# Splitting float32 weights into two float16 halves: GpSimd's subtraction replaced by two TensorE products, and the planner's table drawn anew

## The chip, the cores and the metric

One core of a Trainium2 chip runs the kernel. The metric is device microseconds of one execution, as the median of three runs. Engine names are those of the profile: PE is TensorE (matmuls), PEld its weight loads, DVE is VectorE, ACT is ScalarE, POOL is GpSimd, SP is SyncE, which here issues all DMAs.

## The reference

The inputs are float64. Attention with 8 batches, 8 heads, 576 tokens and a head width of 64 keeps for each query only the 32 largest scores; its output x (4608 tokens by 512) goes through a layer that takes the largest of three products and multiplies it by a fourth matrix.

```
scores = matmul(q, k.T) / sqrt(D)
kth    = partition(scores, -32)[..., -32:-31]
scores = where(scores >= kth, scores, -1e9)
attn   = exp(scores - max) / (sum + 1e-9)
x      = (attn @ v) reshaped to [4608, 512]
h      = max(max(x @ w1, x @ w2), x @ w3)      # w: [512, 768]
out    = h @ w_out                             # [768, 512]
```

## The kernel before

**Units of attention.** The work is cut into units of 128 queries of two heads; 144 units make the 8 batches. A unit goes through all engines: PE makes the scores in PSUM (L518), ACT copies them to SBUF as `ssb` (L526), DVE takes the 8 largest of each of 7 stretches (L535) and a pivot from them (L549 to L567), ACT takes signs against the pivot (L574), POOL multiplies (L579), DVE finds the 32nd largest in the window (L583, L601) and masks with it (L624), ACT takes exponentials (L633), PE transposes them (L679) and multiplies them with v (L710), DVE scales the result (L720). Queries and keys are split into a high and a low part before (L474, L475 on ACT, L479 on POOL).

**The layer behind it** (`mlp`) works on x and the weights as pairs of float16 halves: three products each, high by high, low by high, high by low (L767 for the first stage, L827 for the second). Its pieces are the *fill*: PE takes them where the attention leaves it idle. A part of batch 0's layer can start once its x and the halves of w1, w2 and w3 exist; the last batch's layer mostly runs when the attention is over.

**The weights.** 18 parts of 128 rows are loaded by SP as raw 64-bit words (12 of 768 columns, 6 of 512; L236). `decode` makes float32 of them on DVE with three integer operations for each 384 or 512 columns (L249, L250, L251): 30 times three. ACT squares each part (L261), PE sums the squares by column (L270), DVE takes the largest (L280, L282) and makes a power of two of it as a scale. Then `cut` splits 48 pieces of 256 columns: ACT writes the scaled piece as float32 into `ws` (L307) and as float16 into the place of the high half (L310), POOL subtracts one from the other into the low half (L313). The halves lie in the tile `wall`, over the raw words.

**The order.** Nothing is scheduled by the compiler's own order: `in_order` is a list scheduler with a cost for every piece, a time `GAP` from the end of a piece to its being seen by another engine and `NEAR` on its own, and for each tag a number in `OFFSETS` that is added to its rank (for attention, the unit's number; for the weights, 0). Of the pieces of an engine whose rank is at most `LEAD` above the lowest one it picks the first that could start within `PATIENCE`. Each engine then runs its own list strictly in order. Two rules deal with DVE and POOL: a piece marked `alone` (the masks L624, and L564) is placed after POOL's last piece, and POOL's next one after it:

```
if x.alone:
    t = max(t, free["POOL"] + LOCK_A)
elif x.engine == "POOL":
    t = max(t, shut[0] + LOCK_B)
```

The decode is one DVE piece of three instructions, not marked `alone`. Rings count buffers: `m` has two PSUM banks, for the products of the layer and for the column sums, which take both while a matrix is being decoded.

Of the kernel before, what the change touches and what calls it, by code (L numbers as in the profile page):

```python
# [19 lines left out]
CUT = 256  # L20
# [4 lines left out]
NSSB = 5  # L25
NWB = 6
PMB = 2
GAP = 121.0
NEAR = 87.0
SWITCH = 95.0  # L30
WINDOW = 150
LEAD = 9.1
LOCK_A = -150.0
LOCK_B = -100.0
OFFSETS = {'E0': 1.08, 'E1': 1.7, 'E2': 0.44, 'N': -1.46, 'T0': 0.49, 'T1': 2.25, 'T2': 3.75, 'Y': -0.11, 'Z': 0.23, 'd': 1.26,
           'e': -1.18, 'fin': 3.27, 'g0': -0.91, 'g1': -0.8, 'h': -2.96, 'i': 2.01, 'j': 1.53, 'k0': -0.42, 'k1': 0.33,
           'm0': 0.72, 'm1': 1.14, 'p1': -0.12, 'p2': -0.25, 'p3': -0.74, 'p4': -4.14, 'p5': -1.93, 'q': -1.64, 'ql':
           -5.77, 'qp': -4.75, 'r': -2.3, 's0': 0.4, 's1': 0.16, 'scale': -0.28, 'v': -0.02, 'vl': -11.41, 'vl0': 1.62,
           'vq': 2.42, 'vq0': -3.12, 'w0': 0.96, 'w1': 1.6, 'wc0': 1.74, 'wc1': -1.16, 'wc2': -4.84, 'wd0': -5.89,
           'wd1': -3.67, 'wd2': -0.33, 'wd3': -0.25, 'wl0': -2.77, 'wl1': -2.59, 'wl2': -2.1, 'wl3': 7.51, 'wp0': -3.21,  # L40
           'wp1': -3.82, 'wp2': 2.48, 'wp3': 4.55, 'wq0': -3.26, 'wq1': 3.24, 'wq2': -0.71, 'wq3': 0.18, 'ws0': -6.15,
           'ws1': -1.24, 'ws2': 0.45, 'x0': 0.94, 'x1': 1.58, 'y': 1.99, 'z': 1.41}
# [87 lines left out]
PATIENCE = {'PE': 121, 'DVE': 164, 'ACT': 32, 'POOL': 175, 'SP': 0}  # L130
# [3 lines left out]
def kernel(ctx, tc, q, k, v, moe_w1, moe_w2, moe_w3, moe_w_out, out):  # L134
# [72 lines left out]
    nc.vector.memset(ones_b, 1.0)  # L207
    columns = []
    raw_of = {}

    def halves(i, c, c0, n):

        at0 = 2 * ((i * KC + c) * DF + c0 // CUT * CUT) + c0 % CUT
        return [wall.bitcast(F16)[:, at0 + t * CUT:at0 + t * CUT + n] for t in range(2)]

# [4 lines left out]
    def load_weight(j):  # L220

        src, c, n, at0 = parts[j]
        if c % 2 == 0:
            raw = [wall.bitcast(I32)[:, 2 * CUT + at0:2 * CUT + at0 + 2 * n]]
        elif j < KC:
            k0 = 2 * CUT + N_IN + j // 2 * 2 * n
            raw = [wall.bitcast(I32)[:, k0:k0 + 2 * n]]
        elif j < ODD:
            raw = [t[:, :n] for t in (spare if j % 4 == 1 else [h.bitcast(I32).rearrange("p f n -> p (f n)") for h in H])]
        elif j == len(parts) - 1:  # L230
            raw = [wk.tile([P, 2 * n], I32, name="ssb", bufs=NSSB)]
        else:
            raw = [spare[(j - ODD) // 2]]
# [5 lines left out]
    def decode(j, j0):  # L239

        src, c, n, at0 = parts[j]
        m, k0 = PIECE[n], j0
        raw = raw_of[j]
        if len(raw) == 2:
            raw, k0 = raw[j0 // m:], 0
        raw = raw[0].rearrange("p (n t) -> p n t", t=2)
        low, top = raw[:, k0:k0 + m, 0], raw[:, k0:k0 + m, 1]
        t0, t1 = (io.tile([P, m], I32, name="ob") for _ in range(2))
        nc.vector.tensor_scalar(t0, top, 3, 0x3FFFFFFF, ALU.logical_shift_left, ALU.bitwise_and)  # L249
        nc.vector.scalar_tensor_tensor(t1, low, 29, t0, ALU.logical_shift_right, ALU.bitwise_or)  # L250
        nc.vector.scalar_tensor_tensor(wall.bitcast(I32)[:, CUT + at0 + j0:CUT + at0 + j0 + m], top, -0x40000000, t1,  # L251
                                       ALU.bitwise_and, ALU.bitwise_or)
# [10 lines left out]
    def sum_w(j):  # L263

        c = j % KC
        if c == 0:
            columns[:] = [ps_m.tile([P, 512], F32, name="m") for _ in range(2)]
        squares = squares_of.pop(j)
        for k in range(2):
            nc.tensor.matmul(columns[k][:, :DF // 2], ones_b, squares[:, k * (DF // 2):(k + 1) * (DF // 2)], start=(c == 0),  # L270
                             stop=(c == KC - 1))
# [4 lines left out]
    def column_scale(i):  # L276

        m1 = sm.tile([P, 2], F32, name="m1", bufs=1)
        for k in range(2):
            nc.vector.tensor_reduce(m1[:, k:k + 1], columns[k][:, :DF // 2], AX.X, ALU.max)  # L280
        m2 = sm.tile([P, 1], F32, name="m2", bufs=1)
        nc.vector.tensor_reduce(m2, m1, AX.X, ALU.max)  # L282
# [13 lines left out]

    def cut(j, j0):

        src, c, n, at0 = parts[j]
        w = wall[:, CUT + at0 + j0:2 * CUT + at0 + j0]  # L300
        hi, lo = (wall.bitcast(F16)[:, 2 * (at0 + j0) + t * CUT:2 * (at0 + j0) + (t + 1) * CUT] for t in range(2))
        box = {}

        def scaled():
            box["down"] = scale_of[f"wi{j // KC}" if j < 3 * KC else "wo"][0]
            box["ws"] = io.tile([P, CUT], F32, name="ws", bufs=3)
            nc.scalar.activation(box["ws"], w, AF.Copy, scale=box["down"])  # L307

        def high():
            nc.scalar.activation(hi, w, AF.Copy, scale=box["down"])  # L310

        def low():
            nc.gpsimd.tensor_tensor(lo, box["ws"], hi, ALU.subtract)  # L313
        return scaled, high, low
# [5 lines left out]
                                           rsw=2, pT=1, xs=2, junk=2, books=2, vt=6, x=2, h1=3, ob=2, ws=3).items()}  # L320
# [16 lines left out]
    def weights():  # L337

        decoded, loads, last_cut, release_last, release_spare = {}, {}, [], [], []
        rings["x"].users.append(release_spare)  # L340
        for i in range(4):
# [4 lines left out]
            for j in mine:  # L346
                n = parts[j][2]

                takes = [("ssb", release_last)] if j == len(parts) - 1 else []
                before = {9: (5,), 11: (7,), 12: (1,), 13: (9,), 14: (1, 3), 15: (9,), 16: (3,)}.get(j, ())  # L350
# [803 lines left out]
```

## Time and profile before

| | |
|---|---|
| median of three runs | 1306.12 us (1306.06 to 1307.36) |
| the profiled execution | 1304.12 us, of which the span is 1301.9 us |
| granted TensorE clock over the span | 0.973 |

The profiled execution is 2.0 us under the median; what lies around its span is 2.2 us. The page's strip of 40 slices shows three stages. Here are PE, DVE, POOL and the granted clock, one digit for each 32.5 us, in tenths:

```profile
PE   3435878999789999999999999999999999999997
DVE  7998898999999999999999999999999999999411
POOL 4659688678877888888778787887787787767310
PEclk9997988999689999999999999999999999999999
```

In the first stage, to about 380 us, the weights are decoded and cut, and the first units and batch 0's layer run: DVE is nearly full, PE is not, and its clock is granted in part. In the second, to 1215 us, both are full. In the last, DVE has finished and PE works off what is left of the layer.

### The profile page before, as it was taken

The numbers are of one execution on the slowest core, as the hardware profiler recorded it, in microseconds if no ns is written. First come the engines' busy times: TensorE is split into PE (matmuls) and PEld (weight loads), VectorE is DVE, ScalarE is ACT, GpSimd is POOL, SyncE is SP. The second block draws the span as 40 slices with busy tenths as digits, with TensorE's granted clock in tenths as the row PEclk, the third lists the DMA queues.
The fourth block names the chain that finished last, engine by engine and source line by source line (L and its number), as shares of the span: only waits on it lengthen the run. The fifth ranks groups of instructions, "written<-read, shape, count | busy, mean of one in ns | idle before, by whom it ended". The sixth has DMA issues, their size and how long they took to land.

```text
span 1301.9 us, 31770 instructions
## 1 busy us (share of the span) xinstructions
PE 1174.8 (90%) x10263; PEld 877.3 (67%) x10263; DVE 1174.4 (90%) x5561; ACT 1081.6 (83%) x2438; POOL 954.0 (73%) x1491
## 2 busy tenths in 40 slices
PE   3435878999789999999999999999999999999997
PEld 2223747877568676877777776777677776867775
DVE  7998898999999999999999999999999999999411
ACT  3779988898988899999988998888988898888421
POOL 4659688678877888888778787887787787767310
PEclk9997988999689999999999999999999999999999
DMA  6423112111101101111001111111111111000000
GB/s 200 146 73 109 45 27 47 39 45 37 47 11 28 45 15 50 35 38 47 19 27 39 39 36 42 29 45 29 29 45 28 46 27 37 2 18 2 17 17 28
DMA packets 112399, 54.83 MB, mean 42 GB/s; under 512 B 96608, under 2 KB 104800, under 8 KB 112224
## 3 DMA queue, kind: packets, MB, share of 16 engines
q1 hardware_dynamic: 112224, 52.72, 14.8%
q8 instruction: 83, 1.36, 0.4%
q14 instruction: 92, 0.75, 0.2%
HBM read 43.25 MB, written 9.44 MB: 40 GB/s over the span
## 4 chain that ended last, share of the span: by engine, by line
PE 58%; DVE 13%; ACT 3%; issue 1%; POOL 1%; DMA 0%; SPq 0%; DVEq 0%; POOLq 0%; ACTq 0%
PE m L767 23%; PE tr L710 8%; PE m L827 8%; PE s L518 8%; PE tr L679 7%; DVE L L535 3%; DVE ssb L624 3%; DVE Q L583 2%; PE tr L470 1%; DVE h L776 1%; PE tr L674 1%; ACT pm L633 1%; PE tr L676 1%; DVE z L564 1%; ACT w L574 1%
## 5 line engine op out<-in xcount | busy, mean ns | idle before, releaser
L579 POOL TENSOR_TENSOR w<-ssb,w 128x576 f32<-128x576 f32 x288 | 429.0, 1495 | 56.8 <-ACT w L574 54.2
L767 PE MATMUL m<-xh,wall 128*128 128x256 f16 (+4 forms) x2592 | 440.3, 273 | 2.5 <-DVE h L776 1.7
L767 PEld LDWEIGHTS <-wall 128*128 128x128 f16 x3888 | 352.5, 98 | 75.9 <-issue 11.2
L767 PE MATMUL m<-xl,wall 128*128 128x256 f16 (+4 forms) x1296 | 344.2, 272 | 0.0
L535 DVE MAX8 L<-ssb 128x8 f32<-128x82 f32 (+1 forms) x2016 | 316.3, 228 | 0.2 <-ACT ssb L526 0.2
L624 DVE SCALAR_TENSOR_TENSOR ssb<-ssb,kth 128x576 f32<-128x576 f32 x288 | 256.9, 906 | 1.8
L633 ACT ACTIVATE pm<-ssb,nb 128x576 f32<-128x576 f32 x288 | 223.8, 778 | 26.4 <-DVE ssb L624 25.6
L574 ACT ACTIVATE w<-ssb,Q 128x576 f32<-128x576 f32 x288 | 222.2, 775 | 22.7 <-DVE Q L567 18.8
L691 ACT COPY pT<-tr 128x512 f32<-128x512 f32 (+1 forms) x432 | 215.3, 513 | 22.1 <-PE tr L679 12.9
L583 DVE MAX8 Q<-w 128x8 f32<-128x576 f32 x288 | 215.5, 750 | 6.5 <-POOL w L579 6.3
L679 PE MATMUL tr<-ident,pm 128*128 128x128 f32 x1152 | 183.6, 286 | 24.2 <-ACT pm L633 16.2
L518 PE MATMUL s<-kT,qT 64*128 64x288 f32 x1920 | 179.1, 324 | 20.8 <-ACT ssb L526 11.6
L710 PE MATMUL tr<-pT,vt 128*64 128x256 f32 (+2 forms) x2000 | 182.3, 332 | 4.1 <-ACT pT L691 3.6
L518 PEld LDWEIGHTS s<-kT,qT 64*128 64x128 f32 x1920 | 142.5, 198 | 60.1 <-ACT ssb L526 20.0
L679 PEld LDWEIGHTS tr<-ident,pm 128*128 128x128 f32 x1152 | 133.9, 145 | 68.1 <-ACT pm L633 25.3
L526 ACT COPY ssb<-s 128x1152 f32<-128x1152 f32 x144 | 160.9, 1118 | 14.6 <-PE s L518 13.8
L776 DVE SCALAR_TENSOR_TENSOR h<-m,rises,h 128x256 f32<-128x256 f32 (+4 forms) x216 | 103.0, 477 | 69.0 <-PE m L767 64.7
L710 PEld LDWEIGHTS tr<-pT,vt 128*64 128x64 f32 x2000 | 113.3, 141 | 61.8 <-issue 16.6
L782 POOL TENSOR_TENSOR hl<-h,hh 128x256 f16<-128x256 f32 (+4 forms) x108 | 80.4, 745 | 77.1 <-ACT hh L779 75.8
L827 PE MATMUL m<-wall,hh 128*128 128x512 f16 x432 | 129.2, 380 | 1.6 <-POOL wall L313 1.1
L827 PE MATMUL m<-wall,hl 128*128 128x512 f16 x216 | 82.1, 380 | 0.0
L779 ACT CAST hh<-h 128x256 f16<-128x256 f32 (+4 forms) x108 | 43.6, 404 | 44.4 <-DVE h L776 43.9
(124 smaller groups left out, 1685.4 us busy)
## 6 DMA issues: line engine op xcount, KB each, us to landing
qt<-in_q_dram SPq DMA_DIRECT2D x72, 128.0 KB, 2.8
kt<-in_k_dram SPq DMA_DIRECT2D x72, 128.0 KB, 3.0
out_dram<-ob SPq DMA_DIRECT2D x32, 256.0 KB, 2.3
wall<-in_moe_w_dram SPq DMA_DIRECT2D x8, 768.0 KB, 5.6
vt<-in_v_dram SPq DMA_DIRECT2D x32, 128.0 KB, 2.4
vt<-in_v_dram SPq DMA_DIRECT2D x32, 64.0 KB, 2.2
vt<-in_v_dram SPq DMA_DIRECT2D x96, 16.0 KB, 2.0
vt<-in_v_dram SPq DMA_DIRECT2D x32, 48.0 KB, 2.1
```

What stands on the lines that cost most here:

```text
L518: nc.tensor.matmul(s[:, h, i, :HALF], qT[sl, qa, c0:c0 + P], kT[sl, ka, i * HALF:(i + 1) * HALF], start=(n_ == 0 and a == 0), stop=(n_ == ...
L535: nc.vector.max(d["L"][:, t, g, :], d["ssb"][t][:, g * S // G:(g + 1) * S // G])
L574: nc.scalar.activation(d["w"][t], d["ssb"][t], AF.Sign, bias=d["Q"][:, t, 0:1], scale=-1.0, accum_out=d["cnt"][:, t:t + 1])
L579: nc.gpsimd.tensor_tensor(d["w"][t], d["ssb"][t], d["w"][t], ALU.mult)
L583: nc.vector.max(d["Q"][:, t, 1:NW], d["w"][t])
L624: nc.vector.scalar_tensor_tensor(ss, ss, d["kth"][:, t:t + 1], ss, ALU.is_lt, ALU.subtract, accum_out=d["lost"][:, t:t + 1])
L633: nc.scalar.activation(d["pm"][:, t], d["ssb"][t], AF.Exp, bias=d["nb"][:, t:t + 1], scale=-1.0 / SHRINK, accum_out=d["sums"][:, t:t + 1])
L679: nc.tensor.transpose(pt[:, j * P:(j + 1) * P], pm[:, i, 64 * i + j * P:64 * i + (j + 1) * P], ident)
L691: nc.scalar.copy(pT[:, 512 * i:512 * i + m] if i < 2 else pT[:, 8 * P:10 * P], pt[:, :m])
L710: nc.tensor.matmul(xp[64 * h:64 * h + 64, to], vt[:, 4 * h + i if i < 4 else 8 + h, :], keys, start=(i == 0), stop=(i == 4))
L767: nc.tensor.matmul(box["ps", i][:, :c1 - c0], a, bb[:, kc, c0:c1], start=(kc == 0 and k == 0), stop=(kc == KC - 1 and k == 2))
L827: nc.tensor.matmul(box["po"][:n], a[:, f, cs], bb, start=(f == 0 and k == 0), stop=(f == FC - 1 and k == 2))
```

## The change

- `cut` takes 30 pieces, of 384 columns (w1 to w3) and 512 (w_out). PE multiplies the piece by a diagonal float32 matrix that holds the scale (`times`, one for each weight matrix, made by ACT) into a PSUM bank of the ring `m`; ACT writes the high half as before; PE adds the high half times minus one (`less`, float16) into the same bank; ACT copies the bank into the low half. POOL has no part in it.
- The column sums of both halves of a matrix go into one bank of `m`, so that `column_scale` has one reduction in place of three.
- The three instructions of `decode` are three pieces, each marked `alone`.
- The last part of w_out is staged in the spare tile `xh`, once the part that lay there is decoded, and no longer in an `ssb` buffer.
- `OFFSETS`, `GAP`, `NEAR`, `LEAD` and `PATIENCE` have other values; the first load of a weight and of q and k have tags of their own. A first-stage product of the layer waits for the low halves of all four parts of its matrix, not of two.

```diff
-CUT = 256
+CUT = 512
-GAP = 121.0
-NEAR = 87.0
+GAP = 105.0
+NEAR = 162.0
-LEAD = 9.1
+LEAD = 31.2
-           -5.77, 'qp': -4.75, 'r': -2.3, 's0': 0.4, 's1': 0.16, 'scale': -0.28, 'v': -0.02, 'vl': -11.41, 'vl0': 1.62,
+           -8.08, 'vl0': 7.46, 'vq': 5.8, 'vq0': -2.39, 'w0': 0.34, 'w1': 0.45, 'wc0': -16.48, 'wc1': 1.51, 'wc2':
...
-PATIENCE = {'PE': 121, 'DVE': 164, 'ACT': 32, 'POOL': 175, 'SP': 0}
+PATIENCE = {'PE': 97, 'DVE': 147, 'ACT': 4, 'POOL': 61, 'SP': 0}
...
+    less = const.tile([P, P], F16, name="less")
+    nc.scalar.activation(less, ident, AF.Copy, scale=-1.0)
+    CUTS = {DF: DF // 2, DO: DO}
...
+        def middle():
...
+            nc.vector.tensor_scalar(box["t0"], box["top"], 3, 0x3FFFFFFF, ALU.logical_shift_left, ALU.bitwise_and)
+
+        def end():
+            nc.vector.scalar_tensor_tensor(box["t1"], box["low"], 29, box["t0"], ALU.logical_shift_right, ALU.bitwise_or)
+
+        def front():
...
+        return middle, end, front
...
-            columns[:] = [ps_m.tile([P, 512], F32, name="m") for _ in range(2)]
+            columns[:] = [ps_m.tile([P, 512], F32, name="m")]
...
+        t = times_of[i] = const.tile([P, P], F32, name=f"times{i}")
+        nc.scalar.activation(t, ident, AF.Copy, scale=scale_of[f"wi{i}" if i < 3 else "wo"][0])
...
-        def scaled():
-            box["down"] = scale_of[f"wi{j // KC}" if j < 3 * KC else "wo"][0]
-            box["ws"] = io.tile([P, CUT], F32, name="ws", bufs=3)
-            nc.scalar.activation(box["ws"], w, AF.Copy, scale=box["down"])
+        def whole():
+            box["ps"] = ps_m.tile([P, 512], F32, name="m")
+            nc.tensor.matmul(box["ps"][:, :m], times_of[min(j // KC, 3)], w, start=True, stop=False)
...
+        def rest():
+            nc.tensor.matmul(box["ps"][:, :m], less, hi, start=False, stop=True)
 
         def low():
-            nc.gpsimd.tensor_tensor(lo, box["ws"], hi, ALU.subtract)
+            nc.scalar.copy(lo, box["ps"][:, :m])
```

How the lists of the engines change is shown at three places. The first is the start of SP's list, the DMAs. Before:

```order
L432 DMA qt<-in_q_dram 128x4x64 x2
L432 DMA kt<-in_k_dram 128x4x64 x2
L436 DMA last<-in_q_dram 64x2x64
L436 DMA last<-in_k_dram 64x2x64
L236 DMA wall<-in_moe_w_dram 128x1536 x2
```

Now (`wall`, `xh` and `xl` take weight parts, `qt`, `kt` and `last` the first unit's queries and keys):

```order
L240 DMA wall<-in_moe_w_dram 128x1536 x4
L451 DMA qt<-in_q_dram 128x4x64 x2
L451 DMA kt<-in_k_dram 128x4x64 x2
L455 DMA last<-in_q_dram 64x2x64
L455 DMA last<-in_k_dram 64x2x64
L240 DMA wall<-in_moe_w_dram 128x1536
```

The whole of the first matrix stands ahead of the first unit's queries and keys; it stood behind them, in two halves.

The second place is DVE's list in the decode of the second matrix, while the first units run. Before (L249 to L251 are the decode, L583 to L624 steps of a unit):

```order
L249 TENSOR_SCALAR ob<-wall 128x384
L250 SCALAR_TENSOR_TENSOR ob<-wall,ob 128x384
L251 SCALAR_TENSOR_TENSOR wall<-wall,ob 128x384
L583 MAX Q<-w 128x8
L535 MAX L<-ssb 128x8 x8
L601 TENSOR_REDUCE kth<-oh 128x2
L624 SCALAR_TENSOR_TENSOR ssb,lost<-ssb,kth 128x576 x2
```

Now (L255, L258 and L261 are the decode, L602, L620, L643 and L554 the same steps of a unit):

```order
L255 TENSOR_SCALAR ob<-wall 128x384
L602 MAX Q<-w 128x8
L258 SCALAR_TENSOR_TENSOR ob<-wall,ob 128x384
L261 SCALAR_TENSOR_TENSOR wall<-wall,ob 128x384
L620 TENSOR_REDUCE kth<-oh 128x2
L255 TENSOR_SCALAR ob<-hh 128x384
L643 SCALAR_TENSOR_TENSOR ssb,lost<-ssb,kth 128x576 x2
```

The three instructions of a decode no longer stand in one block; steps of a unit stand between them.

The third place is PE's list where batch 0's layer starts. Before (L767 is its first stage, L679 to L676 are transposes of a unit, L518 is a unit's scores):

```order
L518 MATMUL s<-kT,qT_114 128x288 x12
L679 MATMUL tr<-ident,pm 128x128 x4
L674 MATMUL tr<-ident,pm 128x128
L676 MATMUL tr<-ident,rsw 128x128
L767 LDWEIGHTS wall
L767 MATMUL m<-xh,wall 128x128
```

Now (L786 is the first stage, L322 and L328 the two products of a cut, L698 to L695 the transposes, L537 the scores; `times_1136` is the third matrix's scale):

```order
L328 LDWEIGHTS less
L328 MATMUL m<-wall,less 128x384
L698 MATMUL tr<-ident,pm 128x128 x8
L537 MATMUL s<-kT,qT_115 128x288 x12
L322 MATMUL m<-wall,times_1136 128x384
L693 MATMUL tr<-ident,pm 128x128
L695 MATMUL tr<-ident,rsw 128x128
L786 LDWEIGHTS wall
L786 MATMUL m<-xh,wall 128x128
```

The layer's first products now stand among the cuts of the third matrix. Counted over the list by groups of twelve score products: ahead of the 13th group stood 216 first-stage products, now 12; ahead of the 20th there are 216 in both. Ahead of the 30th stand 444 first-stage and 54 second-stage products before, and 432 and 30 now; ahead of the 42nd 648 and 72 in both.

## Rows read from the trace of the kernel before

**Rows 1.** The page: busy time of each engine over the span

```profile
PE 1174.8 (90%) x10263; PEld 877.3 (67%) x10263; DVE 1174.4 (90%) x5561; ACT 1081.6 (83%) x2438; POOL 954.0 (73%) x1491
```

**Rows 2.** Windows: stretch and its length, busy us of each engine, granted clock, DMA

```profile
0.00:100.00 100.00, 37.42 (x175) 25.67 (x175) 88.25 (x274) 65.38 (x131) 53.89 (x81) 1.00 0.45 138
100.00:200.00 100.00, 70.59 (x621) 52.58 (x621) 90.34 (x392) 90.11 (x216) 81.52 (x120) 0.83 0.21 61
200.00:300.00 100.00, 98.54 (x1028) 81.18 (x1027) 93.81 (x461) 89.05 (x207) 77.50 (x128) 0.98 0.15 39
300.00:380.00 80.00, 62.21 (x471) 43.77 (x470) 76.23 (x391) 71.59 (x164) 64.59 (x101) 0.81 0.15 38
380.00:1215.00 835.00, 826.49 (x7171) 612.77 (x7171) 807.54 (x3999) 745.03 (x1675) 664.83 (x1042) 1.00 0.12 31
1215.00:1302.00 87.00, 79.58 (x805) 61.36 (x802) 18.22 (x51) 20.44 (x51) 11.71 (x23) 0.98 0.06 20
```

**Rows 3.** Timeline of the start: start us, duration us, engine, line, operation

```profile
4.82 1.07 SPq L236 DMA_DIRECT2D wall<-in_moe_w_dram  x2
6.54 0.45 PE L461 MATMUL tr<-ident,last 128*128 128x128 f32 x1 [6.54 <-DMA last<-in_k_dram]
9.51 1.36 DVE L249 TENSOR_SCALAR ob<-wall 128x384 int32<-128x384 int32 x1 [7.97 <-DMA wall<-in_moe_w_dram]
10.61 1.66 POOL L479 TENSOR_TENSOR qT<-raws,qT 128x640 fp32r<-128x640 f32 x1
10.91 1.78 DVE L250 SCALAR_TENSOR_TENSOR ob<-wall,ob 128x384 int32<-128x384 int32 x1
...
13.19 0.35 DVE L249 TENSOR_SCALAR ob<-wall 128x384 int32<-128x384 int32 x1
...
15.04 0.56 DVE L250 SCALAR_TENSOR_TENSOR ob<-wall,ob 128x384 int32<-128x384 int32 x1
...
17.56 2.13 DVE L535 MAX8 L<-ssb 128x8 f32<-128x82 f32 x14
```

**Rows 4.** Timeline of DVE at a part of w_out

```profile
115.58 0.42 DVE L249 TENSOR_SCALAR ob<-wall 128x512 int32<-128x512 int32 x1
116.03 0.69 DVE L250 SCALAR_TENSOR_TENSOR ob<-wall,ob 128x512 int32<-128x512 int32 x1
```

**Rows 5.** Windows of DVE's instructions on the tile `ob`, which are the decode's

```profile
0.00:100.00 100.00, 54.42 (x72) 1.00 0.45 138
100.00:200.00 100.00, 13.45 (x18) 0.83 0.21 61
```

**Rows 6.** Windows of POOL's L313 alone

```profile
0.00:100.00 100.00, 20.85 (x26) 1.00 0.45 138
```

**Rows 7.** Windows of L624 alone, two records for each mask

```profile
100.00:200.00 100.00, 21.02 (x38) 0.83 0.21 61
400.00:1302.00 902.00, 186.66 (x422) 1.00 0.12 31
```

**Rows 8.** Groups by line and form: busy us, mean ns, idle before and its releaser

```profile
L691 ACT COPY pT<-tr 128x512 f32<-128x512 f32 x288 | 165.9, 584 | 13.8 <-PE tr L679 12.9
...
L691 ACT COPY pT<-tr 128x256 f32<-128x256 f32 x144 | 53.0, 371 | 8.3 <-PE tr L676 8.0
...
L313 POOL TENSOR_TENSOR wall<-ws,wall 128x256 f16<-128x256 f32 x48 | 38.2, 800 | 13.2 <-ACT wall L310 12.0
...
L310 ACT ACTIVATE wall<-wall,down_wi 128x256 f16<-128x256 f32 x36 | 17.9, 499 | 0.0
...
L280 DVE TENSOR_REDUCE m<-m 128x1 f32<-128x384 f32 x6 | 3.0, 547 | 0.0
```

**Rows 9.** Chain of waits: start us, us, what (runs of PE products at full clock)

```profile
649.91 1.32 PE m L827 x6
670.45 2.31 PE tr L710 x20
678.58 1.31 PE m L767 x12
```

**Rows 10.** Waits between 0 and 130 us: who, for whom, us, times, longest

```profile
PE m L270 <- ACT junk L261: 39.7, 10, 9.7
```

**Rows 11.** Windows of L767 alone: PE, PEld

```profile
100.00:200.00 100.00, 14.21 (x216) 13.04 (x216) 0.83 0.21 61
```

## What the change should do to the time, predicted from these rows

> **What bounds the kernel now.** The page's busy times [rows 1] don't name a bound: PE and DVE have 90% each. So the windows by stage come next [rows 2]. From 380 to 1215 us PE is busy 826.5 of 835 us at full clock, and DVE 807.5. After 1215 almost only PE has work, 79.6 of 87 us. Up to 380 us DVE has 88.3 + 90.3 + 93.8 + 76.2 = 348.6 us and PE 268.8, at a mean granted clock of 0.83 (100 to 200 us) and 0.81 (300 to 380), between full speed, 2.4 GHz, and half, 1.2.
>
> Between 300 and 380 us PE is idle for 17.8 us: it has caught up, batch 0's layer is done, and it waits for units. What it does from 380 us on is the same list of work whatever happened before, with 8.5 us idle to 1215 and 7.4 after. So the end is the moment at which the units that release batch 1's layer are through, plus a fixed amount of PE work. DVE sets that moment: until then it works through a fixed list of decodes and units. I ask how much earlier DVE can get through the first stage, and whether PE can keep up with 27 us more to do.
>
> DVE's 380 us hold 31.4 us of idle time, 8.0 of it the wait for the first weight load [rows 3], and time in which it counts as busy and is held up. In the timeline of the start [rows 3] a first decode step of 384 columns takes 0.35 us with POOL idle, and the first of all takes 1.36. A second step takes 0.56 us, and 1.78 beside POOL's L479 of 1.66.
>
> **The change part by part.** *Decode.* Alone, the three steps of 384 columns take 0.35 + 0.56 + 0.56 = 1.47 us, the third taken like the second [rows 3]; of 512 columns 0.42 + 0.69 + 0.69 = 1.80 [rows 4]. 24 x 1.47 + 6 x 1.80 = 46.1 us. Measured are 54.4 + 13.5 = 67.9 [rows 5]. So 21.8 us are lost to POOL, the upper bound of what separate `alone` pieces and 38.2 us less of POOL [rows 8] can give. POOL's load falls from 53.9 to 33.0 us in the first 100 [rows 2, 6] and from 81.5 by the other 22 of the 48 subtractions, 17.4, to 64.1. If collisions fell only with the load, to 0.61 and 0.79 of what they were, about 35% of 21.8, 8 us, would come back. A loss can't be excluded either: steps set apart can meet POOL three times and not once, and I put 5 us on it. For the upper end speaks that the masks, planned by the same rule, take 186.7/211 = 0.885 us in the steady part with their second record; against it, that the same masks took 21.02/19 = 1.106 between 100 and 200 us [rows 7], where the lists ran less to plan. Between 8 and 21.8 I take 14.
>
> *Masks in the first stage.* If they fall to the later mean, 19 x (1.106 - 0.885) = 4.2 us [rows 7]. I take 2, between 0 and 4.2.
>
> *Start.* The first load is issued at 4.82 us and the decode starts 4.7 later [rows 3]. Issued first, it goes out at about 0.7, and DVE starts at 5.4, 4.1 us earlier. The price: the first unit's queries and keys stand behind four loads of 0.79 MB; they were there at 6.5 us. 0.79 MB in 4.7 us is 167 GB/s, by which four take 19 us; how far below that they stay no row shows. The first sweep came 11.0 us after the keys and would now come at 31 us at the latest, 22 if the loads take half as long. DVE has cover: the four parts are 8 x 1.47 = 11.8 us, to 17.2, where it used to begin the first unit with four half parts done; scale and next part carry it to about 22. I take 4 less 1 for a gap there: 3, between -5 and 4.
>
> *Column scale.* One of two wide reductions and a small one go: at least 3 x 0.547 = 1.6 us of DVE [rows 8].
>
> *ACT.* It gives up 48 x 2 x 0.5 = 47.9 us (L307 taken like L310 [rows 8]). It gets high halves at 0.61 us for 384 columns and 0.71 for 512 (0.50 at 256 and the slope of L691, 0.213 for 256 columns), copies from PSUM at 0.48 and 0.58, and five small ones of 0.3: 24 x 1.09 + 6 x 1.29 + 1.5 = 35.4. So ACT is 12 us lighter, where it was busy 90 of 100 us [rows 2].
>
> *PE.* The scale products have 24 x 384 + 6 x 512 = 12288 float32 columns. The nearest row is L710: 20 records in 2.31 us [rows 9], which are ten products of 256 columns for two heads in two halves of the array. One after the other that is 0.90 ns a column, two at a time 1.80: 11 to 22 us. The subtraction is float16 at 1.31/12/256 = 0.43 ns a column [rows 9], 5.3 us. I take the upper end, 27.4 us at full clock; at half clock it is twice that.
>
> *New waits.* The second product of a cut waits in PE's list for ACT's high half, and behind it stand transposes and scores of units, which ACT and with it DVE wait for. At about 0.6 us each that is 18 us of PE, most of it at a time when PE waits anyway (39.7 us for squares alone [rows 10]). I charge 2 us to the units. The layer shares the two banks of `m` with the cuts; the order shows its effect: the first 216 products come seven score groups later. Between 0 and 10 us.
>
> Loads ranked anew, the last part's place and the planner's constants I cost at nothing: the lists hold the same work from the 42nd score group on, and there PE is full. If that cover is gone, 1% of that stage is 8 us, either way.
>
> Sum: 14 + 2 + 3 + 1.6 - 2 = 18.6 us off the first stage.
>
> **Can PE bear it?** Its busy time becomes 1174.8 + 27.4 = 1202.2. Its idle time was 62.6 + 29.4 + 1.5 + 17.8 + 8.5 + 7.4 = 127.2 [rows 2]. If units came no earlier: about 14 cuts, 12.8 us, go into the first 100 us and leave 49.8; 14.6 go into the second 100, out of which the layer's 14.2 us [rows 11] and 18 x 0.22 = 4.0 [rows 9] move on, and leave 33.0; these 18.2 take all but 1.1 of the 19.3 idle to 380. With the last two that is 99.8, and 1302.0 in all. So the added work is just swallowed, and what the units gain in the first 200 us comes off idle time that remains. 19 us are to be had, 40 hardly.
>
> Forecast: 1304.1 - 18.6 = 1285.5 for a run like the profiled one, which is 2.0 us under the median; for the median 1287.
>
> **Rivals.** *PE becomes the bound of the first stage (slower).* For it: at the 30th score group 24 x 0.22 + 12 x 0.11 = 6.6 us of the layer are missing. It decides if the cuts of 100 to 200 us run at half clock (14.6 us more) and hold up transposes, so that units come no earlier and PE is still busy with batch 0 when batch 1 is released. Of the 14.6 us about 5 can hide in the lower stage's idle time: 1306 + 10 = 1316; and 1333 if all 27.4 us land in the open. Against it: 62.6 us of idle time in the first 100 us, where half of the cuts stand.
>
> *Only a spare engine is relieved.* POOL has the least to do [rows 1], and collisions only move to other instructions of DVE: 1306 - 1.6 = 1304.5. Against it: 0.35 against 1.36 us for one form [rows 3]. A page would have it so: the Trainium skill, "Perfetto Trace Analysis", section "Identifying the Most-Contended Engine", says to optimise the engine with the highest occupancy and to judge TensorE by its weight loads, not by matmul time. By that, DVE's 90% is the target and POOL's 73% may stay.
>
> *The plan isn't kept.* Collisions fall with POOL's load alone, and the new waits cost 5: 8 + 3 + 1.6 - 5 = 8 us, 1298. For it: the masks' 1.106 us.
>
> *The first stage becomes like the second.* Idle time 3.3% as from 380 to 1215 us [rows 2], no collisions: (348.6 - 21.8 - 4.2) x 1.034 + 5.4 = 339, 41 us less, of which PE allows most: 1266. For it: nothing in DVE's first stage differs but the decode and the start.
>
> **How the numbers follow.** Forecast 0.52, with 1275 to 1298 as its own range; plan not kept 0.12; like the second stage 0.13; spare engine 0.08; PE bound 0.15. A measurement of this kernel can tell 0.2%, 2.6 us, from no change: forecast, plan not kept and like the second stage are faster by more, 0.77; spare engine is the same, 0.08; PE bound is slower, 0.15. The range of 8 in 10 runs from 1269, which leaves out most of the best case, to 1312, which leaves out most of the slower one.
>
> **What would show it.** In the profile after: decode steps near 0.35, 0.56 and 0.56 us, about 54 us in all; DVE's first decode at 5 to 6 us; the last long stretch in which PE idles some 20 us earlier; PE's busy time up by 16 to 27 us and its idle time down by about 45; PE alone at the end for about as long as now. I'd be wrong if decodes still take over 2 us each, if PE has no idle stretch before batch 1's layer, or if the first sweep comes after 31 us.

## The result, and the profile after

The changed kernel takes 1274.88 us (median of four runs, 1273.37 to 1278.8), the kernel before 1306.55 us beside it (1306.06 to 1307.36). The ratio is 0.9762, interval 0.9739 to 0.9784. So 31.7 us are gained where 19 were forecast; 1287 was the forecast, and the range of 1269 to 1312 holds the time.

The profiled execution took 1278.8 us, the longest of its four. It is 25.3 us shorter than the profiled one of before; the other 6.4 us lie between profiled executions and medians. The page's busy times after the change:

```profile
PE 1189.9 (93%) x10353; PEld 877.0 (69%) x10353; DVE 1148.2 (90%) x5555; ACT 1065.2 (83%) x2407; POOL 920.9 (72%) x1443
```

Against [rows 1] PE has 15.1 us more, DVE 26.2 less, ACT 16.4 less, POOL 33.1 less. The stages, with the stretches of [rows 2] where they still fit (length, busy time of PE, PEld, DVE, ACT and POOL, granted clock, DMA):

```profile
0.00:100.00 100.00, 61.26 (x303) 37.56 (x303) 86.21 (x338) 71.07 (x143) 46.58 (x72) 0.83 0.56 175
100.00:200.00 100.00, 85.64 (x756) 61.20 (x755) 89.39 (x422) 92.41 (x215) 73.63 (x109) 0.97 0.13 33
200.00:300.00 100.00, 99.27 (x1034) 80.24 (x1034) 97.54 (x493) 91.68 (x214) 83.32 (x133) 1.00 0.16 40
300.00:360.00 60.00, 43.97 (x364) 31.30 (x362) 57.91 (x306) 56.01 (x129) 49.52 (x75) 0.89 0.14 35
360.00:380.00 20.00, 20.00 (x188) 16.29 (x190) 19.83 (x99) 19.08 (x43) 17.24 (x29) 1.00 0.19 47
380.00:1215.00 835.00, 825.18 (x7173) 610.50 (x7168) 786.47 (x3871) 722.33 (x1637) 643.42 (x1016) 1.00 0.12 31
1215.00:1277.00 62.00, 54.55 (x551) 39.86 (x548) 10.80 (x30) 12.59 (x32) 7.17 (x14) 0.99 0.07 24
```

PE's last stretch with much idle time is now 300 to 360 us, 16.0 us of it, and from 360 us it is full; before, 17.8 us were idle between 300 and 380. So the second stage begins about 20 us earlier. The middle stage is as full for PE as it was.

One column of these rows must be read with care: the granted clock of the start. The trace has its first clock record at 97.7 us before and at 25.9 us after, and the windows count everything ahead of it as full. The transposes L679 of the kernel before show what it was (count; shortest, median and longest duration in ns; first and last start in us), ahead of 97 us, then in a stretch with a granted clock of 0.50, then in one of 1.00:

```profile
L679 PE MATMUL tr<-ident,pm x8: 421/421/476, 37.4 to 39.8; 128*128 128x128 f32 x8
L679 PE MATMUL tr<-ident,pm x4: 421/421/476, 110.1 to 110.8; 128*128 128x128 f32 x4
L679 PE MATMUL tr<-ident,pm x96: 272/273/329, 207.3 to 298.8; 128*128 128x128 f32 x96
```

So PE was at half clock, 1.2 GHz, up to 97.7 us, where [rows 2] and the strip have full clock. In each of the 14 kernels the transposes of this form have a median of 417 to 421 ns ahead of the first clock record and 273 at full clock. Counted so, the mean clock up to the mark defined next is about 0.78 before and 0.88 after (an estimate from the windows and the two first records).

A mark that all kernels have makes this exact: the start of the 36th reduction to `kth` (L601 before, L620 after), one for each unit. It comes at 375.9 us before and at 349.9 after. The windows up to that mark and from it to the end, first of the kernel before, then of the changed one:

```profile
0.00:375.90 375.90, 264.66 (x2262) 200.63 (x2264) 344.73 (x1499) 312.77 (x708) 273.81 (x424) 0.91 0.25 71
375.90:1301.90 926.00, 910.17 (x8005) 676.69 (x8001) 829.66 (x4063) 768.82 (x1731) 680.24 (x1068) 1.00 0.12 30
```

```profile
0.00:349.90 349.90, 282.48 (x2378) 203.88 (x2378) 321.21 (x1513) 302.32 (x678) 245.37 (x374) 0.92 0.27 76
349.90:1276.90 927.00, 907.38 (x7977) 673.08 (x7976) 826.94 (x4042) 762.86 (x1730) 675.51 (x1069) 1.00 0.11 30
```

All 26.0 us come from ahead of the mark, and behind it 1.0 us is lost. Ahead of it DVE is busy 23.5 us less and idle 2.5 us less (31.2 to 28.7). Windows of the decode's tile `ob` alone, to be held against [rows 5]:

```profile
0.00:100.00 100.00, 44.97 (x73) 0.83 0.56 175
100.00:200.00 100.00, 13.48 (x17) 0.97 0.13 33
```

That is 58.5 us against 67.9, 9.4 of the 23.5. Windows of single lines up to the mark give the masks 5.2 us less (65.55 to 60.32, 140 of them), the step marked `alone` beside them (L564, now L583) 2.0 less (12.81 to 10.80) and the column reductions 1.4 less. The other lines do not fall: the sweeps L535 (now L554) rise by 3.0, as 546 of them and not 532 lie ahead of the mark. What is left lies between the lines. The durations of DVE's records, added up, fall by 15.4 us (444.1 to 428.7), and records overlap with the one before them for 107.5 us in place of 99.3; 5.1 of these 8.2 us stand where a decode step and a step of a unit follow each other. The start, in the timeline (start, duration, engine, line, operation, idle time before and its releaser):

```profile
5.20 0.36 DVE L255 TENSOR_SCALAR ob<-wall 128x384 int32<-128x384 int32 x1 [3.66 <-DMA wall<-in_moe_w_dram]
...
15.40 0.35 DVE L255 TENSOR_SCALAR ob<-wall 128x384 int32<-128x384 int32 x1
...
19.93 0.56 DVE L290 TENSOR_REDUCE m<-m 128x1 f32<-128x384 f32 x1 [2.99 <-PE m L281]
...
22.48 1.70 DVE L255 TENSOR_SCALAR ob<-wall 128x384 int32<-128x384 int32 x1
24.21 0.56 DVE L258 SCALAR_TENSOR_TENSOR ob<-wall,ob 128x384 int32<-128x384 int32 x1
...
27.07 1.11 DVE L554 MAX8 L<-ssb 128x8 f32<-128x82 f32 x7 [0.84 <-ACT ssb L545]
```

Eight halves are decoded without a break from 5.20 to 16.9 us, each in the time of a step with POOL idle [rows 3]. The step at 22.48 us shows the other case. Of POOL there stands:

```profile
22.21 1.75 POOL L498 TENSOR_TENSOR qT<-raws,qT 128x640 fp32r<-128x640 f32 x1 [2.43 <-ACT qT L494]
```

DVE's step of 0.35 us begins within POOL's 1.75 us, takes 1.70 and ends 0.22 us after POOL's. [Rows 3] have the like (a decode step beside L479, now L498), and it is still there: the mark `alone` keeps such a step apart from POOL in the plan, and the times of the run differ from the plan's.

### The profile page after: what moved, and what is told of

The parts are those of the page before. It is cut to its first block, busy times and chain, and to the rows that moved or that the text cites. A ratio compares the mean times of both kernels' runs of the same rounds, so it can differ in the third digit from the quotient of the medians.

```text
span 1276.9 us, 31913 instructions
## 1 busy us (share of the span) xinstructions
PE 1189.9 (93%) x10353; PEld 877.0 (69%) x10353; DVE 1148.2 (90%) x5555; ACT 1065.2 (83%) x2407; POOL 920.9 (72%) x1443
## 4 chain that ended last, share of the span: by engine, by line
PE 62%; DVE 23%; ACT 9%; POOL 2%; issue 2%; DMA 0%; DVEq 0%; ACTq 0%; POOLq 0%
PE m L786 25%; PE tr L729 9%; PE m L846 9%; PE s L537 8%; PE tr L698 7%; DVE L L554 6%; DVE ssb L643 5%; DVE Q L602 3%; ACT w L593 2%; DVE h L795 2%; PE tr L489 2%; ACT pm L652 1%; ACT pT L710 1%; ACT ssb L545 1%; PE tr L693 1%
## 5 line engine op out<-in xcount | busy, mean ns | idle before, releaser
L598 POOL TENSOR_TENSOR w<-ssb,w 128x576 f32<-128x576 f32 x288 | 422.3, 1472 | 62.5 <-ACT w L593 57.4
L786 PE MATMUL m<-xh,wall 128*128 128x256 f16 (+4 forms) x2592 | 442.2, 273 | 5.0 <-DVE h L795 2.5
L786 PEld LDWEIGHTS <-wall 128*128 128x128 f16 x3888 | 353.6, 98 | 80.7 <-issue 15.0
L786 PE MATMUL m<-xl,wall 128*128 128x256 f16 (+4 forms) x1296 | 345.5, 273 | 0.0
L554 DVE MAX8 L<-ssb 128x8 f32<-128x82 f32 (+1 forms) x2016 | 317.2, 227 | 2.2 <-ACT ssb L545 2.2
L643 DVE SCALAR_TENSOR_TENSOR ssb<-ssb,kth 128x576 f32<-128x576 f32 x288 | 265.0, 929 | 0.2
L593 ACT ACTIVATE w<-ssb,Q 128x576 f32<-128x576 f32 x288 | 223.7, 778 | 24.3 <-DVE Q L586 18.3
L710 ACT COPY pT<-tr 128x512 f32<-128x512 f32 (+1 forms) x432 | 213.8, 514 | 29.6 <-PE tr L698 10.5
L602 DVE MAX8 Q<-w 128x8 f32<-128x576 f32 x288 | 214.9, 748 | 3.6 <-POOL w L598 3.6
L698 PE MATMUL tr<-ident,pm 128*128 128x128 f32 x1152 | 177.0, 281 | 15.4 <-ACT pm L652 4.4
L537 PE MATMUL s<-kT,qT 64*128 64x288 f32 x1920 | 170.6, 313 | 7.6 <-ACT ssb L545 7.3
L537 PEld LDWEIGHTS s<-kT,qT 64*128 64x128 f32 x1920 | 135.9, 190 | 50.9 <-ACT ssb L545 18.6
L698 PEld LDWEIGHTS tr<-ident,pm 128*128 128x128 f32 x1152 | 131.2, 142 | 53.6 <-issue 19.0
L801 POOL TENSOR_TENSOR hl<-h,hh 128x256 f16<-128x256 f32 (+4 forms) x108 | 83.3, 771 | 89.6 <-ACT hh L798 88.5
```

The lines of the kernel that those rows point to most:

```text
L537: nc.tensor.matmul(s[:, h, i, :HALF], qT[sl, qa, c0:c0 + P], kT[sl, ka, i * HALF:(i + 1) * HALF], start=(n_ == 0 and a == 0), stop=(n_ == ...
L554: nc.vector.max(d["L"][:, t, g, :], d["ssb"][t][:, g * S // G:(g + 1) * S // G])
L593: nc.scalar.activation(d["w"][t], d["ssb"][t], AF.Sign, bias=d["Q"][:, t, 0:1], scale=-1.0, accum_out=d["cnt"][:, t:t + 1])
L598: nc.gpsimd.tensor_tensor(d["w"][t], d["ssb"][t], d["w"][t], ALU.mult)
L602: nc.vector.max(d["Q"][:, t, 1:NW], d["w"][t])
L643: nc.vector.scalar_tensor_tensor(ss, ss, d["kth"][:, t:t + 1], ss, ALU.is_lt, ALU.subtract, accum_out=d["lost"][:, t:t + 1])
```

## The experiments

Times are medians; each ratio is to runs of the kernel before on the same chip. "36th" is the mark above, "behind" the span from it to the end, DVE's columns and the decode are counted up to the mark. The 12 runs in one table, grouped by what they have in common:

| kernel | us | ratio, interval | 36th | behind | DVE busy, idle | decode |
|---|---|---|---|---|---|---|
| before | 1306.5 | | 375.9 | 926.0 | 344.7, 31.2 | 67.9 |
| changed | 1274.9 | 0.976 (0.974-0.978) | 349.9 | 927.0 | 321.2, 28.7 | 58.5 |
| *changed code, POOL free* | | | | | | |
| e8, GAP 106 | 1282.0 | 0.981 (0.979-0.983) | 348.5 | 932.2 | 320.8, 27.7 | 54.8 |
| e11, GAP 104 | 1297.7 | 0.993 (0.991-0.994) | 356.9 | 939.2 | 327.4, 29.5 | 56.4 |
| e9, old numbers | 1281.8 | 0.980 (0.978-0.982) | 351.2 | 929.4 | 317.8, 33.4 | 49.6 |
| e6, keys first | 1290.3 | 0.987 (0.985-0.989) | 354.5 | 932.7 | 321.4, 33.1 | 57.4 |
| e3, decode in one piece | 1293.4 | 0.990 (0.987-0.993) | 356.0 | 934.2 | 325.4, 30.6 | 56.2 |
| e2, scale product twice | 1287.7 | 0.986 (0.984-0.988) | 357.9 | 928.0 | 326.2, 31.7 | 57.2 |
| e4, old numbers, late start | 1309.4 | 1.001 (1.000-1.003) | 376.4 | 931.4 | 324.2, 52.2 | 52.0 |
| *changed code, POOL loaded* | | | | | | |
| e1, POOL load back | 1298.1 | 0.994 (0.991-0.996) | 370.6 | 925.9 | 329.8, 40.8 | 58.0 |
| *code of before* | | | | | | |
| e10, POOL free | 1308.2 | 1.000 (0.999-1.001) | 370.5 | 934.3 | 337.1, 33.4 | 60.7 |
| e12, POOL free, steps apart | 1305.3 | 0.998 (0.997-0.999) | 368.0 | 937.6 | 329.3, 38.7 | 57.8 |
| e7, steps apart | 1307.7 | 1.000 (0.999-1.001) | 380.0 | 925.7 | 349.7, 30.3 | 64.1 |
| e5, new numbers | 1308.7 | 1.001 (1.000-1.002) | 380.5 | 930.6 | 348.2, 32.3 | 66.8 |

**Another plan for the same work (e8, e11).** Only one number of the planner differs:

```diff
-GAP = 105.0
+GAP = 106.0     # e8;  104.0 in e11
```

> The changed kernel with GAP 106 in place of 105: every engine's list is planned anew, and no instruction is added or taken away. It tells how far a new plan alone moves the time. Theory (the gain is DVE time regained in the first stage): the work is the same, so about 1275, within 6 us; decode near 58 us of DVE. Rival (the gain lies in the numbers of the table, drawn to fit): a plan that wasn't searched for loses much of the 31 us, 1285 to 1300.

> The changed kernel with GAP 104 in place of 105: another plan, same work. Theory A (plans that differ by nothing in the work spread by several us, and the table's plan is at the good end): 1276 to 1292 us. Theory B (the 7 us of GAP 106 were a peculiarity of that plan): within 0.2% of the changed kernel, 1272 to 1278 us.

1282.0 and 1297.7 us. The same work in another order costs 7 and 23 us, and most of it behind the mark: 932.2 and 939.2 us against 927.0. For e8 that is between its theory (to 1281) and its rival (from 1285); GAP 104 was outside of what was expected even of a poor plan. This is the yardstick for all that follows: a variant of this kernel that is planned anew differs by some 10 us with no cause in its work, so a difference of that size in one run shows nothing. The mark spreads less (348.5 to 356.9 us, e9 included), and the readings below go by it.

**POOL's load put back, with nobody waiting for it (e1).**

```diff
+            nc.gpsimd.tensor_tensor(v[0], t, v[1], ALU.subtract)   # into a tile that nobody reads
+                    piece("POOL", 3.2 * w, f[4], [h], rank, tag=f"wp{i}")
```

> The changed kernel, with a subtraction on POOL added for each of the 30 cuts (12288 columns, as many as before; its result goes to a tile that nobody reads, and nobody waits for it). The planner knows of it. Theory (collisions with POOL): DVE's decodes, masks and L564's operation lose again part of the 23.6 us of DVE time that the change gave back up to the 36th unit; 8 to 15 us slower than the changed kernel, 1283 to 1290. Rival (ACT's relief or the new table gave the gain, and POOL's load is free): 1275 to 1279.

1298.1 us, slower than the theory's 1283 to 1290, and the mark at 370.6, 14 us outside the spread of plans. Up to the mark:

```profile
0.00:370.60 370.60, 285.04 (x2368) 205.48 (x2370) 329.76 (x1517) 305.48 (x678) 274.57 (x407) 0.90 0.25 72
```

POOL is as loaded as before (274.6 against 273.8). The decode did not get slower (58.0); the masks did (68.5 us, 8.2 more than in the changed kernel), and DVE is idle 12 us longer. What it waits for, the longest two up to the mark (who, for whom, us in total, times, longest):

```profile
DVE xs L746 <- ACT w L600: 6.9, 2, 5.5
DVE Q L609 <- POOL w L605: 6.7, 3, 2.8
```

All of DVE's waits for POOL in that stretch come to 10.9 us, against 2.8 in the changed kernel. POOL, busy 74% of it, costs not only by collisions: units queue behind it.

**The scale product twice (e2).**

```diff
-            nc.tensor.matmul(..., times_of[min(j // KC, 3)], w, start=True, stop=False)
+            for k in range(2):
+                nc.tensor.matmul(..., times_of[min(j // KC, 3)], w, start=True, stop=(k == 0))
```

> The changed kernel, with each cut's float32 scale product done twice into the same bank: 30 products or about 22 to 30 us more of PE, in the first 200 us. Theory (PE has idle time left there, 53 us in the first 200, and 16 more until 360): most is swallowed, 1275 to 1282. Rival (PE bounds the first stage): all of it shows, 1297 or more.

1287.7 us: PE is busy 1206.8 us in all, 16.9 more than in the changed kernel, and 12.8 us slower than it, 5.7 slower than e8. That is between theory and rival. The mark moves by 8.0 us, at the edge of the plans' spread, and the total lies within theirs. So it isn't shown whether PE had room for another 17 us.

**The decode in one piece, not alone (e3).**

```diff
-                    x = piece("DVE", cost[0], steps[0], ..., alone=True, tag=f"wd{i}")
-                    for f, t in zip(steps[1:], cost[1:]):
-                        x = piece("DVE", t, f, [x], rank, alone=True, tag=f"wd{i}")
+                    x = piece("DVE", 1650 if i < 3 else 2000, lambda steps=steps: [f() for f in steps], ...)
```

> The changed kernel with the decode as one piece of three instructions, not marked alone, as it was before. Theory (collisions): the decode's DVE time rises from 58 towards 68 us; 6 to 12 us slower than the changed kernel, 1281 to 1287. Rival (POOL's relief alone removed the collisions): 1275 to 1279, decode still below 60 us.

1293.4 us, the mark at 356.0, the decode at 56.2 us, no more than with separate steps and not "towards 68". With POOL free and the new numbers the separate steps are not what makes the decode shorter (54.8 to 58.5 us with them). That the kernel is 11 us slower than e8 lies in the range of plans.

**Code and numbers exchanged (e4, e5, e9).** e4 is the changed code with the old numbers, e5 the old code with the new numbers, e9 is e4 with two more tags, so that keys and queries come first again. Both also give each matrix's column sums a tile of their own (`columns_of`), as the old ranks let two matrices overlap:

```diff
-            'wl0': -2.77, ...                              # e4
+            'wl': -2.77, 'ql0': -5.77, 'wl0': -2.77, ...   # e9
```

> All of the changed code with the table of before (OFFSETS with 0 for the new tags, GAP, NEAR, LEAD, PATIENCE); the column sums keep one tile for each matrix, as the old ranks let two matrices overlap. Theory (the moved work gives the gain, the table its last 7 us): 1282 to 1292. Rival (the table gives the gain): 1300 or more.

> The kernel before with the new table (OFFSETS, GAP, NEAR, LEAD, PATIENCE), no other change; the tags that only the changed code has play no part, so q, k and the weights are loaded by the ranks of wl0 and ql. Theory (the work makes the gain): not faster than before beyond the spread of plans, 1300 to 1315; decode 65 us or more. Rival (the table): 1285 or less.

> The changed code with the old planner's numbers throughout (OFFSETS, GAP, NEAR, LEAD, PATIENCE); only the first loads get tags of the old ranks, so that keys and queries stand first and the weights follow as in the kernel before. Theory A (the relief of POOL is what saves, the table only fits the plan to it): with a sane start the new code gains under the old numbers too, 1284 to 1296 us; decode 52 to 57 us, DVE busy to the 36th unit 15 to 24 us below before, DVE idle there under 40 us. Theory B (code and table each give nothing alone, the fitted table is what turns the relief into time): 1300 to 1312 us, and DVE's idle time to the 36th unit rises by 15 us or more, as in the run with the old table.

e5 gains nothing (1308.7), as its theory had it. e4 didn't either (1309.4), but for a reason of its own: tags that the old table lacks count as 0, so eight loads went ahead of the keys, and the first decode waited:

```profile
DVE ob L253 <- DMA wall<-in_moe_w_dram: 24.6, 1, 24.6
```

That is 21 us longer than in the changed kernel, while DVE was busy 3 us more than there. e9 removes that and takes 1281.8 us, better than its theory A by time and decode (49.6):

```profile
0.00:351.20 351.20, 278.19 (x2344) 204.09 (x2346) 317.76 (x1487) 301.48 (x673) 238.04 (x374) 0.94 0.26 76
351.20:1280.60 929.40, 914.21 (x8011) 677.71 (x8011) 829.97 (x4069) 769.14 (x1736) 675.68 (x1069) 1.00 0.12 30
```

So the gain is in the code: the new numbers alone give nothing, and under the new code they are worth 7 us, no more than one plan against another. e4 alone would have led to the opposite.

**Keys and queries first (e6).**

```diff
-            'ql0': -6.82, 'wl': -45.21
+            'ql0': -60.0, 'wl': -39.31
```

> The changed kernel with the first unit's queries and keys loaded ahead of the first matrix, as before the change (the rank of ql0 is -60, that of wl is wl0's). Theory: DVE's first decode comes some 4 us later, the first sweep 9 us earlier; the start is worth 0 to 4 us, so with a plan that wasn't searched for, 1280 to 1288. Rival (the early units are what counts, keys first is better): under 1275.

1290.3 us, above the theory's 1280 to 1288, and the first decode waits 7.9 us for its load, 4.2 more; the first sweep comes at 21.95 us, 5.1 earlier and not 9. The mark comes 4.6 us later than in the changed kernel, which agrees, but also lies within the plans' spread; and e9, which starts as e6 does, has it at 351.2. What the start is worth isn't shown by the total. DVE's idle time up to the mark leans the forecast's way: 33.1 and 33.4 us in these two, 27.7 to 29.5 in the three plans with the matrix first (changed, e8, e11).

**Separate steps alone, POOL's relief alone, both (e7, e10, e12).** All three are the code of before with the old numbers. In e7 the decode is three pieces marked `alone`, as in the changed kernel. In e10 POOL fills the low half with zeros (the low halves of the weights are left out), in e12 both are done:

```diff
-            nc.gpsimd.tensor_tensor(lo, box["ws"], hi, ALU.subtract)
+            nc.gpsimd.memset(lo, 0.0)
-                    lo = piece("POOL", 820, f[2], [h], rank, tag=f"wp{i}")
+                    lo = piece("POOL", 150, f[2], [h], rank, tag=f"wp{i}")
```

> The kernel before with the decode in three pieces marked alone, and nothing else: the subtraction stays on POOL. Theory after the last runs (POOL's load is what costs, the marks little): 1298 to 1308, decode still above 60 us. Rival (the marks give the gain): 1290 or less, decode near 55 us.

> The kernel before, but POOL's subtraction is replaced by a fill of the low half with zeros, at a cost of 150 ns in the planner: the low halves of the weights are left out, nothing else is. PE and ACT are as before, only POOL's cut is gone. Theory A (what the change saves is mostly collisions and queueing on POOL): 1284 to 1298 us, decode 52 to 62 us, masks 2 us or more down. Theory B (POOL has time to spare, so its load costs nothing; the gain comes from the new start, the new plan and fewer steps of DVE): 1302 to 1308 us.

> The kernel before with two edits together: POOL's subtraction replaced by a fill with zeros (the low halves are left out), and the decode as three separate pieces, each marked alone. PE, ACT, the start and the table are as before. Each edit alone brought the 36th unit 5 us earlier or 4 later and left the time as it was. Theory A (the two need each other: a decode step set apart from POOL only helps where POOL has room, and room only helps where the steps are set apart): the 36th unit at 350 to 358 us, decode 50 to 57 us, 1283 to 1295 us. Theory B (the rest of the new code is needed too: ACT without the float32 pieces, one column bank, the halves made on PE): the 36th unit at 363 to 372 us, 1297 to 1309 us.

1307.7, 1308.2 and 1305.3 us: none has the gain. e7 is as expected; e10 has the time of theory B, the decode of theory A (60.7), and masks of 65.05 us against 65.55, not 2 less; e12 has time and mark of theory B. e10 and then e12, up to the mark and behind it:

```profile
0.00:370.50 370.50, 263.96 (x2251) 200.16 (x2251) 337.06 (x1488) 310.44 (x701) 247.32 (x421) 0.91 0.25 72
370.50:1304.80 934.30, 916.07 (x8013) 677.00 (x8012) 839.54 (x4075) 771.85 (x1738) 678.55 (x1070) 1.00 0.12 30
```

```profile
0.00:368.00 368.00, 264.30 (x2278) 198.53 (x2280) 329.32 (x1504) 312.09 (x705) 249.56 (x422) 0.85 0.25 73
368.00:1305.60 937.60, 913.00 (x7989) 676.43 (x7985) 845.66 (x4058) 770.27 (x1735) 673.02 (x1069) 1.00 0.11 30
```

POOL's busy time up to the mark is that of the changed kernel (247 and 250 against 245), and DVE's falls by 7.7 and 15.4 us. But the mark comes only 5.4 and 7.9 us earlier, and behind it 8.3 and 11.6 us are lost. In e12 half of DVE's gain turns into waits, in small pieces and for several engines:

```profile
DVE h L785 <- PE m L776: 5.7, 9, 1.5
DVE xs L729 <- PE tr L719: 5.5, 6, 1.9
DVE Q L592 <- POOL w L588: 3.4, 6, 0.7
DVE L L544 <- ACT ssb L535: 2.3, 4, 1.3
```

e9 and e12 have the same numbers, the same order of the first loads and the same decode steps, and POOL is free in both. 16.8 us at the mark are between them, 11.6 of DVE's busy time (8.2 of it the decode) and 5.2 of its idle time. What is left as a difference: ACT is busy 10.6 us less in e9 (no float32 pieces), the column sums have one bank, the pieces are wider, the last weight part has another place, POOL has no fills (15.0 us of them in e12), and PE has 13.9 us more to do, at a granted clock of 0.94 against 0.85 in the rows (about 0.86 and 0.80 with the time ahead of the first clock record, 59.7 and 38.8 us, counted at half). Which of these carries how much was not separated.

## Why the prediction was right, and where its sizes were not

**The bound: right.** The end was to be the moment at which DVE is through the first stage, plus a fixed amount of PE work. The mark came 26.0 us earlier and the span behind it stayed (926.0 and 927.0 us). DVE's last unit even comes 37.7 us earlier (L601 before, L620 after; count, durations, first and last start):

```profile
L601 DVE TENSOR_REDUCE kth<-oh x4: 163/172/172, 1190.3 to 1212.6; 128x2 f32<-128x18 f32 x4
```

```profile
L620 DVE TENSOR_REDUCE kth<-oh x3: 152/156/160, 1163.3 to 1174.9; 128x2 f32<-128x18 f32 x3
```

while the end comes 25.0 us earlier. So PE alone at the end lasts longer by the difference, 12.7 us, not "about as long as now": DVE gained in the second stage too, and there it bought nothing, as PE is what is full. That is this plan's doing: in e9 DVE's last unit comes at 1192.1 us and the end 88.5 later, about as before. How fixed the amount is, was overrated: the same work took 927 to 939 us behind the mark, by plan alone. "If that cover is gone, 1% of that stage is 8 us, either way" was the right price, but it stood beside a cost of nothing and should have stood in the range as a term of its own. That the changed kernel lost only 1.0 us there belongs to one plan, whose numbers were drawn for it, and the prediction had no row for it: e9, e8 and e11 lost 3.4, 6.2 and 13.2.

**The sum: nearly right by luck, and not all of the gain.** The named terms gave 9.4 + 5.2 + 1.4, and 2.5 of idle time: 18.5 us, where 18.6 were forecast. They come so close because the decode was sized too large and the masks too small, and because the 2 us charged for new waits do not show apart. The other 7.5 of the 26.0 us were in no term: L564's 2.0, and DVE records that overlap more, 8.2, less 3.0 for the sweeps.

**Decode, 14 us forecast: 9.4.** The cause was taken to be POOL's load and the separate steps together. e10 gives relief alone 7.2 us of decode, e7 separate steps alone 3.8, e12 both 10.1, e9 18.3. Relief alone is near the lower bound of 8, and e9 near the upper one of 21.8. But the changed kernel and e9 differ by 8.9 us of decode with the same decode pieces, and the two causes don't add up by a rule: e3 shows that separate steps give nothing more under the new numbers, and the 1.70 us step above shows one reason: a step set apart in the plan still meets POOL in the run.

**Masks, 2 us forecast: 5.2, above the upper bound of 4.2.** The bound came from one stretch of 100 us; up to the mark there are 140 masks. The like step beside them gave 2.0. This is the term that was sized too small: collisions were counted for the decode and hardly for the units. POOL's relief alone isn't what gave it: that is 0.5 in e10, 3.6 in e12 and 5.6 in e9 (65.05, 61.94 and 59.99 us).

**Start, 3 us forecast.** The first decode starts at 5.20 us (forecast 5.4, 4.3 earlier than before), there is a gap of 2.99 us for the column sums, and the first sweep comes at 27.07, between 22 and 31 as forecast. DVE's idle time up to the mark fell by 2.5 us only.

**Column scale, 1.6 us: 1.4** for the wide reductions.

**PE, 27.4 us at full clock forecast: 41.3 measured, and yet only 15.1 more in all.** By form (busy us, mean ns of a record, idle before):

```profile
L322 PE MATMUL m<-wall,times 128*128 128x384 f32 x48 | 24.7, 602 | 5.7 <-ACT wall L331 1.8 <-ACT times L310 1.7 <-DMA xh<-in_moe_w_dram 1.3
L328 PE MATMUL m<-wall,less 128*128 128x384 f16 x24 | 7.9, 335 | 5.0 <-ACT wall L325 5.0
L322 PE MATMUL m<-wall,times 128*128 128x512 f32 x12 | 6.4, 619 | 1.3 <-DVE h L795 0.9 <-ACT h L793 0.4
L328 PE MATMUL m<-wall,less 128*128 128x512 f16 x6 | 2.3, 382 | 0.0
```

The float32 product leaves two records, and 24.7 + 6.4 = 31.1 us for 12288 columns are 2.5 ns a column, over the upper end of 1.80 that was taken from L710. The times contain stretches at half clock, but the products of 512 columns all ran at full clock and took 2.1 (6.4 us for 3072). So this term of the forecast was too small. What came back is in the other work: without the cuts' records PE is busy 1157.5 us in all, 17.3 less than before, 14.8 of it up to the mark. The other 8.9 us of the difference are time in which a cut's record stands beside one of other work. Windows of the score products up to the mark, before and then after:

```profile
0.00:375.90 375.90, 57.93 (x516) 0.91 0.25 71
```

```profile
0.00:349.90 349.90, 50.54 (x528) 0.92 0.27 76
```

7.4 us less for 12 records more; the transposes L679 (now L698) take 44.8 us in place of 48.9, the column sums 8.0 in place of 9.6. PE leaves half clock at 25.9 us now, after 97.7 before. Between 100 and 200 us the granted clock is 0.97 now, it was 0.83 [rows 2]: PE had 85.6 us of work there, and 70.6 before, and is at full clock, 2.4 GHz, for nearly all of it. That holds for all runs: in the nine kernels of the changed code the clock of this stretch is 0.91 to 1.00, in the five of the old code 0.82 to 0.85. The prediction took the first 100 us of [rows 2] to be at full clock (12.8 us of cuts), and saw the clock as a price of the cuts and not as something that they give back. PE's idle time fell from 127.2 to 87.0 us, 40 where 45 were forecast.

**New waits, 2 us.** PE waits 5.0 us for ACT's high half (L328 above), and its wait for the squares fell from the 39.7 us of [rows 10] to 22.8:

```profile
PE m L281 <- ACT junk L272: 22.8, 8, 9.1
PE m L328 <- ACT wall L325: 5.0, 7, 1.5
```

Both stand ahead of 130 us, where PE has time.

**ACT, 12 us lighter: 16.4 in all, 10.5 up to the mark.** It was booked as no gain. The comparison of e9 with e12 leaves it as one of the things that may have carried the rest.

**The rivals.** *PE becomes the bound* did not happen, and e2 doesn't show how far it is. *Only a spare engine is relieved* (1304.5) is what the relief alone does: e10 is at 1308.2 beside 1308.1 of before. The rule of the Trainium skill, "Perfetto Trace Analysis", section "Identifying the Most-Contended Engine", agrees with e10. What load costs on an engine that isn't the busiest it doesn't say: in e1 the same POOL load, put back under the changed code, puts the mark 14 to 22 us later. *The plan isn't kept* was put at 1298; e11 has that time (1297.7), but loses it mostly behind the mark, with a decode of 56.4 us, and not to collisions there. *Like the second stage* (1266) was too much: DVE's idle share up to the mark is 28.7 of 349.9, 8%, not 3.3%.

What stays open: how much of the last 17 us up to the mark is ACT's relief, the bank of the column sums or PE's clock, for which no run changes one alone, and why plans of the same work differ by up to 12 us behind the mark.

## What to carry to other kernels

In this pipeline of several nearly full engines the relief of one moved the wait to the next: POOL's relief alone and the separate steps alone gave nothing, both gave 3 us, and the whole change, which also took work from ACT and gave PE more to do early, gave 24 to 32 us under three of its four plans and 10 under the fourth. Where an order is planned by a table of numbers, first measure what a neutral change of one number does (here 7 and 23 us); a single run of a variant that is replanned can't be read below that, and a mark inside the program, behind which the work is the same, reads better than the total. An old table under new code needs care with its new names: missing tags made the first decode wait 21 us longer and hid the whole gain. And a clock that a profile prints is to be checked against durations of one form at its start.

## What was not expected of the hardware

With more TensorE work in the first stage the rest of TensorE's work was shorter, as its granted clock rose (0.82 to 0.85 between 100 and 200 us in all five kernels without the products, 0.91 to 1.00 in all nine with them). Up to the trace's first clock record TensorE ran at half clock in all 14, though the windows print 1.00 there. It left half clock at 23.3 to 65.6 us with the products and at 79.7 to 107.4 without them, in e12 at 38.8. The clock was not changed by itself, so what it is worth in the time isn't shown. A DVE step of 0.35 us that began 0.27 us after a POOL instruction of 1.75 us took 1.70; POOL's ended at 23.96 us and DVE's at 24.18. A POOL fill of 128x256 float16 took 0.31 us where the subtraction of that size took 0.80 [rows 8].
